# Unit 0's last fills shortened, one k load put off, unit 1's normalizations all on VectorE, weight loads held while unit 5's rows are transposed

## The chip, the cores and the metric

The kernel runs on one core of one Trainium2 chip. The metric is the device time of one execution in microseconds (us); the figure to compare is the median of several executions.

## The reference

Two layers, each a gated convolution followed by a gated feed-forward block, over 2048 tokens of width 576 in bfloat16:

```
x = x + A(layernorm(x));  x = x + B(layernorm(x))      # twice, the same weights
A(q) = q * (causal_conv(kv, ssm_k) + kv * ssm_D)       # by FFT over the 2048 tokens
       kv = (4-tap shift of A_k) * A_v
B(x) = (gelu(x @ w_gate) * (x @ w_up)) @ w_down        # 576 -> 4608 -> 576
```

kv does not depend on x, so the convolution's result y is computed once and used by both layers.

## The kernel before

**Tiles.** The tokens are cut into four blocks c of 512 (four rows-of-128, j = 0 to 3). A unit is one layer of one block: units 0 and 1 are layer 0 of blocks 0 and 1, units 2 and 3 layer 1 of the same blocks; units 4 and 5 are layer 0 of blocks 2 and 3, units 6 and 7 their layer 1. The passes over the weights are `[[0], [1, 2], [3, 4], [5, 6], [7]]`. Each pass has three phases (a third of the 4608 hidden columns each); a visit is one unit in one phase.

**A visit** is 12 gate/up groups (L1635: 18 products each of 64x512, gate and up into one PSUM pair), whose Gelu runs on ScalarE and whose product hT = gelu(gate) * up runs on VectorE (L1645), and then four row blocks of down products (L1669: 24 products each), each added to x_c by VectorE. In unit 0 VectorE is short of time, so while convolution work of block 1 is left, the groups go in twos: ScalarE takes both halves out of PSUM (L1542, L1543) and VectorE makes one 128x1024 product for two groups (L1546, in `hidden`). That product waits in the list `made` until `run_made` issues it. Unit 0's first phase takes its rows in two halves (`half_gu`).

**The convolution** of block m runs beside all this: transforms of k*v and of the filter on TensorE (the four steps of `quarter`, L292, for each half h of the columns; a step is two products), their evictions on ScalarE, complex products and sums on VectorE (the queue V), inverse transforms on TensorE (L416), and a spill of the spectra through HBM. `filt(m)` transforms block m of the filter, `step(m)` does the rest. Their TensorE work is the queue `Pq`, in order; it is offered within the down products, and within gate/up groups only where `now()` says so (for `quarter`, only the last two steps of the second half). y of block 1 is wanted by unit 1, y of block 2 by unit 4, y of block 3 by unit 5.

**A unit's rows** are made by `gate2_steps` (two VectorE operations a row, L1236 and L1243: x + (x - mean) * y * rstd), then a mean on GpSimd (L1193), a square on ScalarE (L1201), two small GpSimd operations for rstd (L1208, L1209), the normalization xn (on ScalarE, L1265, in `norm`; or on VectorE, L1273 and L1275, in `norm_v`), and two transposing DMAs on SyncE's queue (SP) into xnT (L1298, in `spread`). The unit's first gate/up product needs all four rows of xnT.

**The order** on every engine is written out by a planner: `Pace` keeps a time for TensorE, VectorE and ScalarE, moved on by constants (`C_GU` = 1.944 for a gate/up group, `C_DN` = 0.245 for two down products, and so on). After each group or pair of down products, `fill(limit, ...)` issues what is ready: weight loads (`weights`), loads of the convolution (`run_loads`), transposes (`spreads`), products in `made` that are ready, VectorE work as long as the planned VectorE time stays below `limit`, ScalarE work, and convolution steps on TensorE. `limit` is the planned TensorE time plus C_GU plus LEAD (1.8), or HURRY (2.6) while y of block 1 is unfinished. The engines then run their own lists in order, each at its own speed; a DMA that must wait holds up what is behind it on its queue.

**Weight loads** are entered with a due time (`when_due`) once the group that frees their buffer is planned: three DMAs (L1155 to L1157) on SP, the same queue as the transposes. `weights()` issues them all at once, except that while unit 1's rows are being made and turned, those due more than HOLD = 14 us ahead are kept back.

**k and v** of block 2 are loaded on GpSimd's queue (`lk` in `step`, L174). `conv.clear` lets `lk` and the steps of `filt` go as soon as all four of unit 1's rows have their transposes issued.

Of the kernel before, what the change touches and what calls it, by code (L numbers as in the profile page):

```python
# [26 lines left out]
RT = BS // P  # L27
# [4 lines left out]
NEVER = 1e9  # L32

C_GU, C_DN = 1.944, 0.245
# [7 lines left out]
AHEAD, CHAINED = 2.0, 2.5  # L42
LATE = (1, 2)
HOLD, LEAD, HURRY, SPARE = 14.0, 1.8, 2.6, 4.0


def twiddles():
# [1050 lines left out]
def ssm_geglu_kernel(ctx, tc, A_q, A_k, A_v, A_shift_k, A_ssm_k, A_ssm_D, B_x, B_w_gate, B_w_up,  # L1098
# [9 lines left out]
    FP = FT // NP  # L1108
# [13 lines left out]
    t = Pace()  # L1122
# [54 lines left out]
    aq, nq = deque(), deque()  # L1177
# [80 lines left out]
    def prep(ui, j):  # L1258
        layer, c = units[ui]
        v = nvars.setdefault(ui, [{"pfx": "l_"} for _ in range(RT)])[j]  # L1260

        def norm(ready):
            xn = xnp.tile([P, XW], BF16, tag="xn", name="xn")
            for lo, hi in ((0, D), (D, XW)):
                nc.scalar.activation(out=xn[:, lo:hi], in_=x_c[c][:, j, 0:hi - lo], func=ACT.Identity,  # L1265
                                     scale=v["rstd"][:, 0:1], bias=v["nb"][:, 0:1])
            xn_made.append((ui, j, xn, t.on_act(C_NA, max(ready, t.pe - 1.0)) + 0.3 - 2.0 * (ui == 1)))

        def norm_v(j):
            def run():  # L1270
                v = nvars[ui][j]
                xn = xnp.tile([P, XW], BF16, tag="xn", name="xn")
                nc.vector.tensor_scalar(out=xn[:, 0:D], in0=x_c[c][:, j, :], scalar1=v["nm"][:, 0:1],  # L1273
                                        scalar2=v["rstd"][:, 0:1], op0=ALU.add, op1=ALU.mult)
                nc.vector.tensor_copy(out=xn[:, D:XW], in_=xn[:, 0:HK])  # L1275
                xn_made.append((ui, j, xn, t.dve + C_NV - 1.7))
            return ("v", nvars[ui][j], "rstd_at"), C_NV, run
        tasks = gate2_steps(c, j, (hvars if layer else gvars)[c][j], v, layer == 1)
        if ui > 1 or j == 1:
            v["norm"] = norm  # L1280
        if ui == 1:
            tasks += [norm_v(i) for i in {1: (0,), 3: (2, 3)}.get(j, ())]
        return tasks

    hvars = {}
# [7 lines left out]
    xn_made = deque()  # L1293
# [11 lines left out]
        blk_of[2 * b + 1] = 5 + b  # L1305

    vq = deque()
    xnT_of, xn_done = {}, {}

    def run_vq(limit, till=0.0):  # L1310
        if not vq:
# [19 lines left out]
    def spreads():  # L1331
        while xn_made and xn_made[0][3] <= t.pe:
            ui, j, xn, _ = xn_made.popleft()
            if ui not in xnT_of:
                xnT_of[ui] = xtp.tile([P, NKC, CH], BF16, tag="xnT", name="xnT")
            spread(xnT_of[ui], j, xn)
            xn_done[ui] = xn_done.get(ui, 0) + 1

    due = []

# [3 lines left out]

    def turns_near():

        return bool(xn_made or nq) or 1 in xnT_of and xn_done.get(1, 0) < RT

    def weights():

        while due:
            near = turns_near() and xn_done.get(1, 0) < RT
            if near and due[0][0] > t.pe + HOLD:
                break
            _, _, load, n = due.pop(0)
            load(n)
# [19 lines left out]
    def fill(limit, tensor, conv_first):  # L1376
        weights()
        conv.run_loads()
        spreads()
        while made and made[0][0] <= max(t.pe + 0.2, t.dve):  # L1380
            run_made()
        while True:
            if conv_first:
                if not (conv.run_v(limit) or run_vq(limit)):
                    break
            else:
                done = run_vq(limit)
                if done is None or not (done or conv.run_v(limit)):
                    break
        while run_aq(min(limit, t.pe + 2.3)):  # L1390
            pass
        conv.flush(t.pe)
        if tensor and (hurry() or t.pe > conv.last + (CHAINED if chained() else 0.0)):
            for _ in range(3):
                if not conv.run_p():
                    break
        if unit0 and conv.borrowed:
            while run_vq(limit, t.pe + C_GU):
                pass

    with tc.manual_schedule():
# [133 lines left out]
        def hidden(dst, pair, e, count):  # L1535
# [11 lines left out]
                    out=dst, in0=ga[:].rearrange("p e (f q) -> p (e f) q", f=count), in1=dst, op=ALU.mult)))  # L1547
            return when + 0.1

        def half_gu(hT, n, half, old):  # L1550
            pair = psp.tile([P, 2, 512], F32, tag="pr", name="gu")
            xnT, tok = xnT_of[0], slice(half * 2 * P, (half + 1) * 2 * P)
            for e in range(2):
                w, gi = wgu[(2 * n + e) // FG], (2 * n + e) % FG
                for k in range(NKC):
                    for s, r0 in ((0, 0), (1, HK)):
                        nc.tensor.matmul(pair[:, s, e * 256:(e + 1) * 256], lhsT=w[r0:r0 + HK, k, gi * P:(gi + 1) * P],  # L1557
                                         rhs=xnT[r0:r0 + HK, blk_of[k], tok], start=(k == 0), stop=(k == NKC - 1))
            if not old:
                return lambda: hidden(hT[:, 4 * (n // 2):4 * (n // 2) + 4, tok], pair, n % 2, 2)  # L1560
            ga = work.tile([P, CH], F32, tag="ga", name="ga")
            nc.scalar.activation(out=ga[:], in_=pair[:, 0, :], func=ACT.Gelu_apprx_tanh)
            nc.vector.tensor_tensor(out=hT[:, 2 * n:2 * n + 2, tok], in0=ga[:].rearrange("p (e q) -> p e q", e=2),
                                    in1=pair[:, 1, :].rearrange("p (e q) -> p e q", e=2), op=ALU.mult)
# [20 lines left out]
            return kind is not None and need[0] == "y2" and need[1:3] not in conv.y_at  # L1585
        now = lambda: wanted() or hurry() and (t.pe > 60.0 or conv.fresh > 0)
        conv.tight, conv.turning = chained, turns_near
        conv.clear = lambda: 0.0 if xn_done.get(1, 0) >= RT else NEVER
        visits = []
        for pi, us in enumerate(passes):  # L1590
            visits += [(pi * NP + ph, ph, ui, k == 0, k == len(us) - 1)
# [1 line left out]
        for wb, ph, ui, first, final in visits:  # L1593
            layer, c = units[ui]
            while xn_done.get(ui, 0) < RT:
                if not run_vq(t.pe + 3.0):
                    conv.run_loads()
                    run_aq(t.pe + 3.0)
                    conv.run_v(t.pe + 1.5)
                    conv.run_p()  # L1600
                    t.pe += 0.2
                spreads()
            for kind, n in at_start.get((ui, ph), []):
                if kind == "es":
                    act_early(n)
                elif kind == "x":
                    load_x(n)
                else:
                    for j in range(RT):
                        vq.extend(prep(n, j))  # L1610
# [8 lines left out]
            if wb == 0:  # L1619
                first_half(hT)  # L1620
                for n in range(FP // 2):
                    tail = half_gu(hT, n, 1, False)
                    t.pe = max(t.pe, free.popleft()) + C_GU
                    free.append(tail())
                    if n % 2:
                        when_due(t.pe, load_wgu, n // 2 + 3)
                    fill(t.pe + C_GU + (HURRY if hurry() else LEAD), now(), conv.left > 0)
            for fi in range(FP if wb else 0):
                n, gi = divmod(wb * FP + fi, FG)
                w = wgu[n]  # L1630
                pair = psp.tile([P, 2, 512], F32, tag="pr", name="gu")
                for k in range(NKC):
                    b = blk_of[k]
                    for s, r0 in ((0, 0), (1, HK)):
                        nc.tensor.matmul(pair[:, s, :], lhsT=w[r0:r0 + HK, k, gi * P:(gi + 1) * P],  # L1635
                                         rhs=xnT[r0:r0 + HK, b, :], start=(k == 0), stop=(k == NKC - 1))
                t.pe = max(t.pe, free.popleft()) + C_GU
                if ui == 0 and (fi % 2 and rounded or fi % 2 == 0 and conv.left > 0):
                    rounded = True
                    free.append(hidden(hT[:, fi - fi % 2:fi - fi % 2 + 2, :], pair, fi % 2, 1))  # L1640
                else:
                    rounded = False
                    ga = work.tile([P, CH], F32, tag="ga", name="ga")
                    nc.scalar.activation(out=ga[:], in_=pair[:, 0, :], func=ACT.Gelu_apprx_tanh)  # L1644
                    nc.vector.tensor_tensor(out=hT[:, fi, :], in0=ga[:], in1=pair[:, 1, :], op=ALU.mult)  # L1645
                    free.append(t.on_dve(C_HT, t.on_act(C_GELU, t.pe + 0.15) + 0.15) + 0.1)
                if conv.borrowed:
                    free.popleft()
                    free.append(conv.borrowed)
                    conv.borrowed = None  # L1650
                if gi == FG - 1 and final:
                    when_due(t.pe + (FP - FG) * C_GU + 12.0, load_wgu, n + 3)
                fill(t.pe + C_GU + (HURRY if hurry() else LEAD), now(), conv.left > 0)
            conv.borrowed = None
            while made:
                run_made()
# [103 lines left out]
```

## Time and profile before

| | us |
|---|---|
| median of 3 runs (920.41 to 921.9) | 921.73 |
| the profiled execution, its own time | 919.29 |
| its span, first to last instruction | 917.5 |
| TensorE busy (98% of the span) | 902.6 |
| VectorE busy (63%) | 577.1 |
| ScalarE busy (36%) | 334.3 |
| GpSimd busy (17%) | 160.1 |
| granted TensorE clock | 1.0 throughout |

By the chain that ended last, an undisturbed gate/up of 12 groups takes 23.42 us and an undisturbed set of down products 11.87 us, with 0.49 us more for every four products of the convolution between them. The landmarks of that chain used below: unit 0's second phase begins at 80.42, its third at 117.25, that phase's down products at 144.94; unit 1's gate/up begins at 161.04, its down products at 184.69; unit 4's last phase begins at 560.38, its down products at 583.8; unit 5's gate/up begins at 595.59. All times in the texts are from the span's start.

### The profile page before, as it was taken

How to read it: one execution, taken by the hardware profiler on the slowest of the kernel's cores; microseconds unless marked ns; L12 is line 12 of the kernel's file. 1: busy time of each engine (PE TensorE's matmuls, PEld its weight loads, DVE VectorE, ACT ScalarE, POOL GpSimd, SP SyncE). 2: the span in 40 equal slices, each digit the busy share in tenths (PEclk: the TensorE clock that was granted, in tenths of full speed). 3: DMA queues.
4: the chain of work that ended last, by engine and by line, in shares of the span. 5: the costliest groups of instructions: out<-in, count | busy, mean ns of one | idle time of the engine just before them, and what ended most of it. 6: DMA issues, size and time to landing. Idle time of an engine off the chain costs nothing.

```text
span 917.5 us, 19235 instructions
## 1 busy us (share of the span) xinstructions
PE 902.6 (98%) x8166; PEld 526.5 (57%) x8166; DVE 577.1 (63%) x983; ACT 334.3 (36%) x628; POOL 160.1 (17%) x334
## 2 busy tenths in 40 slices
PE   8899998999999999999999999999999999999998
PEld 6786555465565564654655655656546556556555
DVE  7989877768889884697898865442332335332332
ACT  6865546523224145353124133551121224421211
POOL 3503405220114022340113002220000003100000
PEclk9999999999999999999999999999999999999999
DMA  9979997948518609893925802940720821977620
GB/s 253 332 198 281 246 251 122 207 155 168 181 53 202 167 1 151 239 155 83 277 68 118 192 16 59 179 126 5 151 78 2 155 79 27 164 174 174 138 63 27
DMA packets 128955, 131.15 MB, mean 143 GB/s; under 512 B 43618, under 2 KB 120675, under 8 KB 128868
## 3 DMA queue, kind: packets, MB, share of 16 engines
q1 hardware_dynamic: 119232, 93.47, 49.1%
q0 software_dynamic: 9632, 36.43, 12.3%
q8 instruction: 64, 1.05, 0.5%
q14 instruction: 23, 0.19, 0.1%
q10 hardware_dynamic: 4, 0.01, 0.0%
HBM read 108.35 MB, written 11.80 MB: 131 GB/s over the span
## 4 chain that ended last, share of the span: by engine, by line
PE 92%; DVE 3%; DMA 2%; ACT 1%; SPq 1%; POOL 1%; issue 0%; DVEq 0%; POOLq 0%; ACTq 0%
PE gu L1635 58%; PE dn L1669 28%; PE gu L1557 2%; DMA xnT<-xn 2%; PE ps L217 1%; PE cps L292 1%; PE ps L416 1%; PE cps L416 1%; SPq L1298 0%; PE ps L292 0%; DVE wx L948 0%; DVE x_c L1460 0%; DVE x_c L1457 0%; POOL rstd L1209 0%; PE cps L885 0%
## 5 line engine op out<-in xcount | busy, mean ns | idle before, releaser
L1635 PE MATMUL gu<-xnT,wgu 64*128 64x512 bf16 x4968 | 541.0, 376 | 4.1 <-DMA xnT<-xn 4.1
L1635 PEld LDWEIGHTS <-wgu 64*128 64x128 bf16 x4968 | 241.5, 94 | 297.0 <-issue 10.5
L1644 ACT ACTIVATE ga<-gu 128x512 f32<-128x512 f32 x258 | 154.0, 597 | 467.8 <-PE gu L1635 460.8
L1645 DVE TENSOR_TENSOR hT<-ga,gu 128x512 bf16<-128x512 f32 x258 | 177.0, 686 | 205.0 <-ACT ga L1644 203.5
L1669 PE MATMUL dn<-wd,hT 128*128 128x288 bf16 x2304 | 292.2, 286 | 1.4 <-DVE hT L1546 1.4
L1669 PEld LDWEIGHTS <-hT 128*128 128x128 bf16 x2304 | 223.4, 98 | 67.2 <-issue 9.5
L1705 DVE TENSOR_TENSOR x_c<-x_c,dn 128x576 f32<-128x576 f32 x64 | 48.1, 752 | 61.4 <-PE dn L1669 61.2
L1193 POOL TENSOR_SCALAR nm<-s 128x1 f32<-128x1 f32 x60 | 20.4, 340 | 273.4 <-DVE x_c L1700 210.9
L1201 ACT ACTIVATE junk<-x_c,nm 128x576 bf16<-128x576 f32 x48 | 36.9, 768 | 22.4 <-POOL nm L1193 21.0
L1209 POOL TENSOR_TENSOR rstd<-ve,neghalf_t 128x1 f32<-128x1 f32 x62 | 41.9, 676 | 5.2
L556 POOL DMA_DIRECT2D hr<-Hd x32 | 17.4, 545 | 123.5 <-DVE prod L375 122.3
L1208 POOL TENSOR_SCALAR ve<-ss 128x1 f32<-128x1 f32 x62 | 25.3, 408 | 57.5 <-ACT junk L1201 57.3
L1265 ACT ACTIVATE xn<-x_c,nb,rstd 128x576 bf16<-128x576 f32 (+1 forms) x50 | 29.7, 644 | 4.8 <-POOL nb L1213 4.8
L1691 DVE TENSOR_TENSOR ob<-x_c,dn 128x576 bf16<-128x576 f32 x15 | 11.3, 754 | 30.2 <-PE dn L1669 27.2
L1542 ACT ACTIVATE ga<-gu 128x512 bf16<-128x512 f32 x26 | 15.5, 597 | 33.4 <-PE gu L1635 26.4
L295 ACT COPY eo<-cps 128x576 f32<-128x576 f32 x29 | 18.6, 640 | 20.4 <-PE cps L292 16.8
L1557 PE MATMUL gu<-xnT,wgu 64*128 64x256 bf16 x432 | 24.6, 269 | 0.1
L431 POOL DMA_DIRECT2D out_dram<-ob x12 | 6.8, 565 | 94.4 <-DVE ob L1691 74.2
L376 DVE TENSOR_TENSOR prod<-prod 128x576 bf16<-128x576 bf16 x48 | 22.0, 458 | 1.7
L1557 PEld LDWEIGHTS <-wgu 64*128 64x128 bf16 x432 | 20.8, 94 | 3.5 <-issue 0.7
L255 DVE SCALAR_TENSOR_TENSOR eo<-eo 128x576 f32<-128x576 f32 x22 | 16.4, 752 | 4.7 <-ACT eo L295 4.7
L616 DVE TENSOR_TENSOR zs<-sum,prod 128x576 f32<-128x576 bf16 x24 | 18.1, 754 | 0.4
(164 smaller groups left out, 581.1 us busy)
## 6 DMA issues: line engine op xcount, KB each, us to landing
wgu<-in_B_w_gate_dram SPq DMA_DIRECT2D x45, 576.0 KB, 6.0
wd<-in_B_w_down_dram SPq DMA_DIRECT2D x30, 864.0 KB, 6.9
wgu<-in_B_w_up_dram SPq DMA_DIRECT2D x45, 512.0 KB, 7.9
hr<-Hd POOLq DMA_DIRECT2D x32, 288.0 KB, 5.0
kr<-Kd POOLq DMA_DIRECT2D x24, 288.0 KB, 5.4
Kd<-kc POOLq DMA_DIRECT2D x12, 288.0 KB, 7.3
k<-in_A_k_dram POOLq DMA_DIRECT2D x3, 1008.0 KB, 13.2
wgu<-in_B_w_up_dram SPq DMA_DIRECT2D x45, 64.0 KB, 7.4
```

The source lines that it names most:

```text
L376: nc.vector.tensor_tensor(out=dst, in0=pr[:, 0, :], in1=pr[:, 1, :], op=ALU.subtract if part == 0 else ALU.add)
L1193: nc.gpsimd.tensor_scalar(out=v["nm"][:], in0=v["s"][:], scalar1=-1.0 / D, scalar2=None, op0=ALU.mult)
L1201: nc.scalar.activation(out=junk[:], in_=get_x(), func=ACT.Square, bias=v["nm"][:, 0:1], accum_out=v["ss"][:])
L1208: nc.gpsimd.tensor_scalar(out=ve[:], in0=v["ss"][:], scalar1=1.0 / D, scalar2=EPS, op0=ALU.mult, op1=ALU.add)
L1209: nc.gpsimd.tensor_tensor(out=v["rstd"][:], in0=ve[:], in1=neghalf_t[:, 0:1], op=ALU.pow)
L1265: nc.scalar.activation(out=xn[:, lo:hi], in_=x_c[c][:, j, 0:hi - lo], func=ACT.Identity, scale=v["rstd"][:, 0:1], bias=v["nb"][:, 0:1])
L1557: nc.tensor.matmul(pair[:, s, e * 256:(e + 1) * 256], lhsT=w[r0:r0 + HK, k, gi * P:(gi + 1) * P], rhs=xnT[r0:r0 + HK, blk_of[k], tok], sta ...
L1635: nc.tensor.matmul(pair[:, s, :], lhsT=w[r0:r0 + HK, k, gi * P:(gi + 1) * P], rhs=xnT[r0:r0 + HK, b, :], start=(k == 0), stop=(k == NKC - 1))
L1644: nc.scalar.activation(out=ga[:], in_=pair[:, 0, :], func=ACT.Gelu_apprx_tanh)
L1645: nc.vector.tensor_tensor(out=hT[:, fi, :], in0=ga[:], in1=pair[:, 1, :], op=ALU.mult)
L1669: nc.tensor.matmul(part[h][:, h, 0:HW], lhsT=hT[:, fi, at * P:(at + 1) * P], rhs=wd[2 * wb + fi // WT][:, fi % WT, h * HW:(h + 1) * HW], s ...
L1705: nc.vector.tensor_tensor(out=xh, in0=xh, in1=acc[:, :, 0:HW], op=ALU.add)
```

## The change

Four parts, all in the planner's rules; no operation changes its shape.

1. **Ends of unit 0's gate/up.** `lead(left)` sets the limit of the fill: with a product in `made` and fewer than two groups left, VectorE may be filled only to 1.5 us (ENDING) past the planned TensorE time after the last group, where it was C_GU + 2.6 or 1.8. And the loop that issues unit 1's gating right after two inverse transforms (`conv.borrowed`) gets a limit of its own, C_GU + 1.6 (VISIT) counted from after those transforms, where it had the fill's limit, counted from before them.
2. **k of block 2** and the steps of `filt` wait until 9 us (LANDED) after unit 1's last row was issued for transposing (`xn_at`), in planned time.
3. **Row 1 of unit 1** is normalized by `norm_v` on VectorE, as rows 0, 2 and 3 are; it stands behind row 3's gating, ahead of rows 2 and 3.
4. **Weights held back also for unit 5**: from unit 4's last phase on, `turning` holds unit 5 too, and `weights()` and `turns_near()` go by the units in it whose rows are not all turned.

```diff
+LANDED, ENDING, VISIT = 9.0, 1.5, 1.6
...
-        if ui > 1 or j == 1:
+        if ui > 1:
             v["norm"] = norm
         if ui == 1:
-            tasks += [norm_v(i) for i in {1: (0,), 3: (2, 3)}.get(j, ())]
+            tasks += [norm_v(i) for i in {1: (0,), 3: (1, 2, 3)}.get(j, ())]
...
             xn_done[ui] = xn_done.get(ui, 0) + 1
+            xn_at[ui] = t.pe
...
-        return bool(xn_made or nq) or 1 in xnT_of and xn_done.get(1, 0) < RT
+        return bool(xn_made or nq) or any(u in xnT_of for u in left_to_turn())
+
+    turning = [1]
+
+    def left_to_turn():
+        return [u for u in turning if xn_done.get(u, 0) < RT]
...
         while due:
-            near = turns_near() and xn_done.get(1, 0) < RT
+            near = turns_near() and left_to_turn()
             if near and due[0][0] > t.pe + HOLD:
                 break
...
         if unit0 and conv.borrowed:
-            while run_vq(limit, t.pe + C_GU):
+            while run_vq(t.pe + C_GU + VISIT, t.pe + C_GU):
                 pass
...
+        def lead(left):
+
+            if made and left < 2:
+                return ENDING + left * C_GU
+            return C_GU + (HURRY if hurry() else LEAD)
...
-        conv.clear = lambda: 0.0 if xn_done.get(1, 0) >= RT else NEVER
+        conv.clear = lambda: xn_at[1] + LANDED if xn_done.get(1, 0) >= RT else NEVER
...
+            if (ui, ph) == (4, 2):
+                turning.append(5)
...
-                    fill(t.pe + C_GU + (HURRY if hurry() else LEAD), now(), conv.left > 0)
+                    fill(t.pe + lead(FP // 2 - 1 - n), now(), conv.left > 0)
...
-                fill(t.pe + C_GU + (HURRY if hurry() else LEAD), now(), conv.left > 0)
+                fill(t.pe + lead(FP - 1 - fi if ui == 0 else FP), now(), conv.left > 0)
```

More of the change, by code (lines that the diff above doesn't have):

```diff
@@ L1307, in ssm_geglu_kernel @@
     vq = deque()
-    xnT_of, xn_done = {}, {}
+    xnT_of, xn_done, xn_at = {}, {}, {}
     def run_vq(limit, till=0.0):
```

## The prediction

> **What bounds the kernel now.** I read the page first: TensorE is busy for 902.6 of 917.5 us at a granted clock of 1.0, so time comes only from its idle stretches or from the work in its list, and the change takes no product away. So I asked next for what TensorE waits for. Two rows after the opening 45 us matter:
>
> ```profile
> PE gu L1635 <- DMA xnT<-xn: 4.1, 2, 3.2
> PE dn L1669 <- DVE hT L1546: 1.4, 1, 1.4
> ```
>
> Three waits in all: two on transposed rows, one on VectorE. The chain of waits in order of time places them, and busy time over windows cut at its landmarks prices them (columns: window, length, busy PE, PEld, DVE, ACT, POOL, then clock, DMA share, GB/s):
>
> ```profile
> 80.42:117.25 36.83, 35.46 (x315) 19.66 (x316) 32.37 (x56) 18.63 (x40) 14.35 (x25) 1.00 1.11 291
> 144.94:157.86 12.92, 12.92 (x106) 10.09 (x104) 9.45 (x22) 9.35 (x20) 7.18 (x19) 1.00 0.86 134
> 157.86:161.04 3.18, 0.00 (x0) 0.03 (x1) 1.41 (x4) 0.55 (x2) 1.59 (x4) 1.00 0.52 114
> 161.04:184.69 23.65, 23.64 (x217) 10.51 (x218) 17.76 (x30) 12.83 (x25) 6.31 (x13) 1.00 0.96 195
> 560.38:583.80 23.42, 23.42 (x217) 10.44 (x218) 14.09 (x24) 13.92 (x27) 6.59 (x17) 1.00 0.68 131
> 595.59:620.12 24.53, 23.66 (x218) 12.26 (x218) 11.51 (x21) 13.62 (x27) 6.19 (x17) 1.00 0.48 122
> 620.12:631.99 11.87, 11.87 (x99) 9.32 (x100) 2.95 (x4) 0.60 (x1) 0.00 (x0) 1.00 0.00 0
> ```
>
> An undisturbed gate/up is 23.42, undisturbed down products 11.87. So unit 0's second phase loses 36.83 - 35.29 = **1.54**; from 144.94 to 184.69 are 39.75 against 23.42 + 11.87 + 0.98 (eight convolution products in between), **3.48** lost; unit 5 loses 24.53 - 23.42 = **1.11**. The sum, 6.13 us, is the most that this change can bring.
>
> **Part 1, the ends of gate/up.** The timeline at the end of unit 0's second phase:
>
> ```profile
> 104.37 0.58 ACT L1543 CAST hT<-gu 128x512 bf16<-128x512 f32 x1
> 104.52 1.43 DVE L390 TENSOR_TENSOR yb<-zs 128x576 bf16<-128x576 f32 x2
> 105.86 0.75 DVE L373 TENSOR_TENSOR prod<-kr,H 128x1152 bf16<-128x1152 bf16 x1
> 107.03 0.68 DVE L1546 TENSOR_TENSOR hT<-ga,hT 128x1024 bf16<-128x1024 bf16 x1
> 107.76 9.48 PE L1669 MATMUL dn<-wd,hT 128*128 128x288 bf16 x76 [1.37 <-DVE hT L1546]
> ```
>
> ScalarE is done with the last pair at 104.95, but VectorE first does 2.5 us of convolution (L390, L373, L376). With 1.5 us of fill the product goes at 104.95 and ends at 105.65; TensorE needs it after 20 down products, at 106.39. The wait goes whole: **-1.54**. The 2.5 us move behind the product; no VectorE work is added, and VectorE stood idle in those down products for 0.76 and 0.98 us waiting for TensorE (L1705) and 0.89 at 121.5 (for ScalarE), which takes up the 1.5 us that TensorE gains on it. If that cover is short, the chain to the inverse transforms (L397 ends at 129.83, the transforms start at 132.83: 3.0 us to spare, 1.6 after the gain) would miss its place by one group, 1.95 us. In the first phase's end the same rule only reorders; no wait stands there.
>
> The second half of this part: after the first pair of inverse transforms VectorE does row 0's gating, then waits 1.16 us (to 137.68) for Gelu, though y of row 1 is out at 135.65; after the second it waits 1.11 (to 141.86). Counted from after the transforms (1.96 us by the planner's constant) with 1.6 instead of 2.6, the limit is 0.96 later, room for one more 0.82 operation each time. Rows 1 to 3 come up to 1 us sooner. The hT product behind them slips by some 0.4 us; it frees a PSUM pair wanted two groups later.
>
> **Part 3, row 1's norm.** ScalarE loses two L1265 (1.19 us together), GpSimd one L1213 (0.19); VectorE gains L1273 and L1275, 0.57 + 0.18. Behind row 3's gating it would run at 146.9 to 147.7 (VectorE is idle there, 1.17 us to 148.09), 1 us after ScalarE's. Queued behind it: rows 2 and 3's norms, which start no later than now (148.78 and 149.48, behind L1705's sister L1700 at 148.09), and sooner if anything, since their squares no longer wait behind L1265. Eight transposing DMAs remain, 1.27 us each on SP: row 1 147.7 to 150.2, row 2 to 152.7, row 3 to 155.3.
>
> **Part 2, k of block 2.** SP's and GpSimd's rows, and DMA around them:
>
> ```profile
> 140.77 15.96 SPq L1298 DMA_TRANSPOSE xnT<-xn  x8
> 151.66 0.64 POOL L174 DMA_DIRECT2D k<-in_A_k_dram  x1
> 152.00:154.00 2.00, 2.00 (x18) 1.60 (x17) 1.67 (x5) 1.09 (x3) 0.87 (x4) 1.00 1.10 93
> 154.00:156.00 2.00, 2.00 (x19) 1.58 (x17) 1.14 (x3) 1.15 (x3) 1.75 (x5) 1.00 0.94 339
> ```
>
> Rows 0 and 1 land 2.5 to 2.6 us after issue. The second DMA of row 2 (issued 150.84) took 6.9 and the last (154.30) 7.1, its issue 2.43 instead of 1.27, while k's 1008 KB moved at 339 GB/s. With k away, the last DMA, issued near 154.0, lands by 156.5. The down products then end at 144.94 + 11.87 = 156.81, for the filter's steps leave too: the 3.48 go whole, margin 0.3, or about 1.3 with the sooner rows. Bounds: 3.48 down to 1.5, if the last rows land as slowly as 5 us.
>
> [...] In the two windows above the rate says that k had nearly all; the trace speaks against an even split here.
>
> What is moved: eight filter products (0.98 us) from 150 to 155 into unit 1's down products from 184.69, which then hold sixteen. Unit 2's, from 220.95 to 234.78, hold sixteen now and take 13.83 = 11.87 + 1.96, no wait. Zero. k was landed at 160.15 and first used at 174.49; issued from 158.8 with a landing of 8.5 to 13.4 (its three issues), it is there by 172.2: 2.3 to spare (on GpSimd's queue it only goes behind the x_b load of 159.29); gone, VectorE waits with hT products behind it. The v load (GpSimd, 188.03) waits for the filter's second half, some 6.5 us later now (two halves take 9.4 from 221.14 to 230.5, one 2.5), and v is used at 200.86: the convolution of block 2 slips by 4 to 8 us. Its last shift (L397) ends at 325.03; the filter's next half begins at 328.95 in down products that last to 342.59. It still gets in.
>
> **Part 4, unit 5.**
>
> ```profile
> 576.06 0.61 SPq L1155 DMA_DIRECT2D wgu<-in_B_w_gate_dram  x1
> 578.75 6.68 SPq L1298 DMA_TRANSPOSE xnT<-xn  x4
> 585.53 0.60 SPq L1155 DMA_DIRECT2D wgu<-in_B_w_gate_dram  x1
> 587.59 9.79 SPq L1298 DMA_TRANSPOSE xnT<-xn  x4
> ```
>
> Row 1's xn is ready at 573.93, but SP stands waiting for the weights' buffer till 576.06 and turns the row at 578.75; row 3's, ready at 581.69, goes at 587.59 behind another load and lands 8 us later. Held back, rows 2 and 3 go at 579.7 to 584.9 and land by 593 even with that 8: **-1.11**. The weights: due 27.55 us after the freeing group, kept until 14 before; the first is then issued about 13.5 us late in the planner, 10 or more before its use, landings being 6.0 to 7.9.
>
> **Sum**: -1.54 - 3.48 - 1.11 = -6.13, so the profiled 919.29 becomes 913.2. The median shown stands 2.44 above that execution; I carry the difference over: 921.73 - 6.13 = 915.6, and with some 0.3 for small new waits, **915.9**.
>
> **Rivals.**
> (a) *The last rows still land late.* For it: three causes must all go (k, SP's 1.27 each, the order in VectorE), the margin is 0.3 to 1.3, and z could miss its place by one group. [...]
> (b) *Nothing gained*: the planner's new order shifts the waits elsewhere, 920.5 to 922.5. Against it: each wait has one named releaser that the change touches.
> (c) *Slower, by the convolution.* If block 2's chain slips by more than 17 us (325.03 to 342.59), the filter's half falls to the next down products, 365.94, 37 us on. Then block 3's last shift comes at 576 instead of 538.93 and misses the down products of 546.55; its inverse transforms run in unit 4's last gate/up, unit 5's gating begins at 577 instead of 563.70, 13.3 later. The rows' last landing, 587 to 593 by part 4, becomes 601 to 606, 5 to 11 after the 595.59 at which TensorE wants them, while 5.0 of the gain stay: 921.8 to 927.4, say 925. For it: the sixteen products and v's wait. Against it: I get 4 to 8 of the 17.
> (d) *The hold does nothing* for unit 5: 1.11 stay, within the forecast's range.
>
> **Numbers.** Forecast (and d), 914.3 to 917.2: 0.58. (a) to 919.5: 0.20. (b): 0.08. (c): 0.14. The lower end is the full sum (915.6) less 1.3, what the lowest run shown lies below the median: 914.3. The range reaches through (a) to the faster edge of (b), 920.8. About 0.2%, 1.84 us, is what a measurement can tell from no change: faster 0.78, same 0.08, slower 0.14.
>
> **What would show it.** The row of waits for L1546 is gone and hT is made right after the last L1543; unit 1's gate/up begins right at the end of the down products, k's issue behind the last transpose; four L1273 where three stood and 48 L1265 where 50; unit 1's down products take 13.8; SP's transposes of unit 5 lie together, weights behind. I am wrong if a new wait of over 1 us stands in TensorE's rows, above all one on xnT near 590 or on y's chain.

## The result and the profile after

| | median us | lowest to highest | executions |
|---|---|---|---|
| before | 921.82 | 920.41 to 921.93 | 4 |
| after | 913.81 | 913.24 to 914.72 | 4 |

The ratio is 0.9918, with a 95% interval of 0.99 to 0.9935: 8.0 us, or 0.8%, less. The median lies 2.1 below the 915.9 of the forecast and 0.5 below the lower end of its range. The changed kernel's profiled execution took 914.25, its span 912.5, at a mean granted clock of 0.998.

All that TensorE waits for in the changed kernel, over the whole span (line that waits, line it waits for, us in total, times, longest):

```profile
PE xps L1436 <- DVE xn L1420: 2.7, 1, 2.7
PE cps L241 <- DVE v L943: 1.3, 1, 1.3
PE cps L886 <- DVE wx L864: 1.2, 1, 1.2
PE ps L899 <- ACT sx L901: 0.7, 1, 0.7
```

These four lie in the first 36 us and were there before. The rows on xnT and on hT are gone: behind the opening, TensorE waits for nothing any more. The windows that answer to those of before (unit 0's second phase; its last down products; unit 1's gate/up; its down products; unit 5's gate/up; line numbers have moved by 15, so L1650 is the gate/up and L1684 the down products):

```profile
81.21:116.49 35.28, 35.28 (x314) 19.68 (x316) 32.19 (x55) 18.61 (x40) 15.32 (x25) 1.00 1.08 292
...
144.25:156.12 11.87, 11.87 (x100) 9.29 (x100) 8.15 (x20) 6.10 (x14) 6.29 (x16) 1.00 0.57 78
156.12:179.54 23.42, 23.42 (x218) 10.46 (x218) 15.73 (x28) 13.17 (x27) 7.25 (x19) 1.00 1.01 245
179.54:193.36 13.82, 13.82 (x114) 10.86 (x116) 10.13 (x19) 5.31 (x9) 0.78 (x2) 1.00 0.15 44
...
591.49:614.91 23.42, 23.42 (x217) 10.46 (x218) 11.43 (x21) 13.62 (x27) 6.17 (x17) 1.00 0.89 170
```

Every stretch now has the undisturbed length: 36.83 became 35.28, unit 5's 24.53 became 23.42, and unit 1's gate/up starts where the down products end. From the start of those down products to the end of unit 1's gate/up it is 179.54 - 144.25 = 35.29 instead of 39.75; 0.98 of the difference came back as the filter's eight products in unit 1's down products, 13.82 instead of 12.84. So 1.55 + 3.48 + 1.11 = 6.14 were taken out of TensorE's time, to within 0.01 of the forecast's sum.

VectorE at the end of unit 0's second phase (start, duration, line):

```profile
104.65 0.76 DVE L617 TENSOR_TENSOR zs<-sum,prod 128x576 f32<-128x576 bf16 x1
105.77 0.69 DVE L1553 TENSOR_TENSOR hT<-ga,hT 128x1024 bf16<-128x1024 bf16 x1 [0.37 <-ACT hT L1550]
106.38 1.42 DVE L391 TENSOR_TENSOR yb<-zs 128x576 bf16<-128x576 f32 x2
107.72 0.75 DVE L374 TENSOR_TENSOR prod<-kr,H 128x1152 bf16<-128x1152 bf16 x1
```

The last hT no longer stands behind L391, L374 and the product that follows: it waits 0.37 for ScalarE, and they come after it. SyncE's queue ahead of unit 5:

```profile
567.77 6.17 SPq L1299 DMA_TRANSPOSE xnT<-xn  x4
574.04 0.64 SPq L1156 DMA_DIRECT2D wgu<-in_B_w_gate_dram  x1
574.73 0.62 SPq L1157 DMA_DIRECT2D wgu<-in_B_w_up_dram  x1
575.40 0.63 SPq L1158 DMA_DIRECT2D wgu<-in_B_w_up_dram  x1
576.13 7.01 SPq L1299 DMA_TRANSPOSE xnT<-xn  x4
583.24 0.60 SPq L1156 DMA_DIRECT2D wgu<-in_B_w_gate_dram  x1
```

Two groups of four transposes with one set of weights between them, where two sets stood (the forecast had none); the last is issued by 583.2, 8.3 before unit 5 begins. One thing does not fit, though: the two profiled executions differ by only 919.29 - 914.25 = 5.0, less than the 6.14 taken out (0.79 of it is lost ahead of unit 0's second phase, which begins at 81.21 and not at 80.42), while the medians differ by 8.0. That gap is what the experiments had to explain.

### The profile page after: what moved, and what is told of

It is laid out like the page before. It is cut to its first block, busy times and chain, and to the rows that moved or that the text cites. A ratio compares the mean times of both kernels' runs of the same rounds, so it can differ in the third digit from the quotient of the medians.

```text
span 912.5 us, 19232 instructions
## 1 busy us (share of the span) xinstructions
PE 903.1 (99%) x8166; PEld 525.6 (58%) x8166; DVE 577.4 (63%) x985; ACT 333.0 (36%) x626; POOL 160.0 (18%) x333
## 3 DMA queue, kind: packets, MB, share of 16 engines
q8 instruction: 64, 1.05, 0.5%
## 4 chain that ended last, share of the span: by engine, by line
PE 98%; DVE 1%; ACT 0%; issue 0%; DVEq 0%
PE gu L1650 59%; PE dn L1684 31%; PE gu L1570 3%; PE cps L293 1%; PE ps L417 1%; PE ps L218 1%; PE cps L417 1%; PE ps L293 0%; DVE wx L949 0%; PE xps L1436 0%; PE cps L886 0%; DVE wx L952 0%; PE cps L218 0%; DVE x_c L1467 0%; DVE x_c L1464 0%; PE ps L963 0%
## 5 line engine op out<-in xcount | busy, mean ns | idle before, releaser
L1650 PE MATMUL gu<-xnT,wgu 64*128 64x512 bf16 x4968 | 540.7, 377 | 0.0
L1650 PEld LDWEIGHTS <-wgu 64*128 64x128 bf16 x4968 | 240.3, 94 | 293.7 <-issue 5.9
L1684 PE MATMUL dn<-wd,hT 128*128 128x288 bf16 x2304 | 292.3, 287 | 0.0
L1684 PEld LDWEIGHTS <-hT 128*128 128x128 bf16 x2304 | 223.1, 98 | 65.9 <-issue 9.5
```

What stands on the lines that cost most here:

```text
L1684: nc.tensor.matmul(part[h][:, h, 0:HW], lhsT=hT[:, fi, at * P:(at + 1) * P], rhs=wd[2 * wb + fi // WT][:, fi % WT, h * HW:(h + 1) * HW], s ...
```

## The experiments

Every kernel here was timed beside the kernel before on the same chip, and the ratios are against that. Four chips were used in all; on them the kernel before's executions with a mean granted clock of 0.996 have medians from 921.16 to 922.12, so a difference of less than 1 us between two kernels timed on different chips is not sure. Line numbers differ a little from kernel to kernel.

**The kernel before, again.** Twice, unaltered: 12 executions (b1) and a single one (b2). Two theories of the 2.44 between the profiled execution and the median were put to it.

> The kernel before once more, unchanged, for a second profile of it and for what its executions differ by. The profiled execution of before took 919.29, the median 921.8. Theory V (the waits vary): a second profiled execution shows the same three waits, of another length, above all the one on xnT at unit 1 (3.2 in the first) or unit 5 (0.9), and an execution near 922 has 2 to 2.5 more there. Theory S (the start): the three waits are the same within 0.3 and the 2 us lie in the first 66 us, by a granted clock under 1 there, as the changed kernel's profile has at 36 to 39 us. Ratio to before 0.998 to 1.002 by both.

> The kernel before a third time, one look. V: the wait on xnT at unit 1 is again another, between 3 and 6. S: all three waits as in the first profile within 0.3, the first 66 us differ.

Measured: b1 921.51 median (917.25 to 923.53, 12 executions), ratio 0.9993 (0.9979 to 1.0008), profiled 922.14 at a clock of 0.996; b2 922.06, profiled, clock 0.996. TensorE's waits are nearly those of the first profile: 3.7 and 3.5 at unit 1 where it had 3.2, 0.5 and 0.8 at unit 5 where it had 0.9, 1.4 for hT in both. That is at most 0.5 more at unit 1 where theory V asked for 2 to 2.5 more in all, so V falls. The clock is what differs. Windows of b1 behind the wait at unit 1 (the column behind POOL's count is the granted clock):

```profile
157.00:160.40 3.40, 0.80 (x7) 0.39 (x5) 2.16 (x4) 1.35 (x4) 1.79 (x5) 1.00 1.31 50
160.40:163.80 3.40, 2.32 (x12) 1.03 (x14) 0.00 (x0) 0.00 (x0) 0.00 (x0) 0.50 1.17 217
163.80:167.20 3.40, 3.40 (x19) 1.41 (x16) 0.96 (x2) 1.35 (x3) 0.16 (x1) 0.50 1.10 226
```

The same window in the kernel before's first profile:

```profile
163.80:167.20 3.40, 3.40 (x34) 1.56 (x32) 3.03 (x6) 2.32 (x6) 2.01 (x6) 1.00 1.10 224
```

TensorE is "busy" for 3.40 us in both, but it gets through 19 products in the one and 34 in the other. The trace's clock record has b1 at half clock from 160.42 for 6.83 us, b2 from 162.21 for 3.41 and, at the start, from 35.92 for 3.41; the first profile has no such stretch ahead of the last products. b1's unit 1 gate/up took 26.31, b2's 25.17, against 23.64 in the first profile and 23.42 undisturbed. Theory S, which put the loss into the first 66 us, holds for one of b2's two stretches and for none of b1's. So the profile that the forecast was worked out from was the uncommon case.

**k held back alone, and everything but k.** `only_k` is the kernel before with part 2 alone, `no_k` the changed kernel without it:

```diff
# only_k, on the kernel before
+LANDED = 9.0
...
+            xn_at[ui] = t.pe
...
-        conv.clear = lambda: 0.0 if xn_done.get(1, 0) >= RT else NEVER
+        conv.clear = lambda: xn_at[1] + LANDED if xn_done.get(1, 0) >= RT else NEVER
# no_k, on the changed kernel: the last line back
```

> Before with part 2 alone (k of block 2 and the filter's steps 9 us after unit 1's last row). If k's transfer is what holds the last rows: unit 1's wait of 3.2 (5 or more in a typical execution) falls below 0.7, the last row's transposes land 2.5 to 3 after issue; time 3 to 5 below before. If the rows come late by themselves (the rival): 1.5 or more of the wait stays and the time is within 2 of before. The waits of 1.37 on hT and 0.87 at unit 5 stay in both.

> After without part 2: k and the filter's steps go as soon as unit 1's rows are issued. If k is the cause: the wait on xnT at unit 1 comes back, 2 to 4 us, and the time is 916 to 918. If the sooner rows (parts 1 and 3) are enough: no wait over 0.5, time 913 to 914.5, and in that case part 2 buys nothing.

Measured: only_k 917.18 (915.75 to 917.62, 5 executions), ratio 0.9955 (0.9939 to 0.9971); no_k 918.51 (915.93 to 919.89, 10), ratio 0.9966 (0.9954 to 0.9979). no_k's median lies 0.5 above the range expected of it; it has a half-clock stretch at the start and one at unit 1. only_k has no wait at unit 1 left; no_k has one of 3.5, and the stretch from 161.44 for 3.41 behind it. What the transposes issued from 148.0 on (146.8 in only_k, 147.1 in no_k) took to land (min, median, max), for the kernel before, then only_k, then no_k:

```profile
L1298 SPq DMA_TRANSPOSE xnT<-xn x5: 1199/1265/2433, 148.0 to 154.3; - x5
...
DMA to landing us min/median/max: 2.5/6.9/7.1
```

```profile
L1299 SPq DMA_TRANSPOSE xnT<-xn x6: 1199/1261/2148, 146.8 to 154.4; - x6
...
DMA to landing us min/median/max: 2.5/2.5/4.1
```

```profile
L1299 SPq DMA_TRANSPOSE xnT<-xn x5: 1201/1264/2735, 147.1 to 154.0; - x5
...
DMA to landing us min/median/max: 2.5/7.5/7.6
```

The issue times hardly differ, the landings do: with k's 1008 KB in flight on GpSimd's queue the last transpose lands 7.1 (before) and 7.5 (no_k) after its issue at 154.3 and 154.0, without it (only_k, issued at 154.4) 2.5, and the slowest 4.1. That is why rival (a) did not come: k was the cause of nearly all of the wait, as the forecast had it, and not of a part of it. The rate that the prediction read this from does not show it by itself, since the transposes have few bytes to move. The trace also has the packets: between 150 and 156.8 in the kernel before, k's queue moved 0.98 MB in 135 of them and SyncE's 0.33 MB in 1353, so one packet of k holds as much as 30 of a transpose (7.3 KB against 0.24). No run tests whether the slow landings have to do with that. Part 2 is the larger half of the change.

**The other parts, each left out of the changed kernel.** `no_hold` without part 4, `no_lead` without the smaller fill, `no_rows` without the limit VISIT and without row 1's norm on VectorE:

```diff
# no_hold
-            if (ui, ph) == (4, 2):
-                turning.append(5)
# no_lead
-            if made and left < 2:
-                return ENDING + left * C_GU
# no_rows
-        if ui > 1:
+        if ui > 1 or j == 1:
-            tasks += [norm_v(i) for i in {1: (0,), 3: (1, 2, 3)}.get(j, ())]
+            tasks += [norm_v(i) for i in {1: (0,), 3: (2, 3)}.get(j, ())]
-            while run_vq(t.pe + C_GU + VISIT, t.pe + C_GU):
+            while run_vq(limit, t.pe + C_GU):
```

> The changed kernel without its fourth part: unit 5's weights are not held back. Theory C (the prediction's three waits, and a half-clock stretch of 3.41 us only behind a TensorE idle of some 3 us): unit 5's wait of 1.1 us comes back and nothing else, since 1.1 us of idle is too short to bring a slow stretch: 914.8 to 915.0 median. Rival 1: any wait brings a slow stretch, then 1.1 + 1.7 = 2.8 more, 916.6. Rival 2: the rows of unit 5 come early enough without the hold, then 913.8 and no wait.

> The changed kernel without the smaller fill at the ends of unit 0's gate/up. Theory C: the wait of the down products for the last hT of unit 0's second phase is back, 1.4 us, with no slow stretch behind it: 915.2 to 915.4 median. Rival 1 (any wait brings a slow stretch): 1.4 + 1.7, 916.9. Rival 2: the new order of VectorE's work (the visits) already takes the convolution's operations out of that place, then no wait and 913.8.

> The changed kernel with unit 1's rows made as in the kernel before (row 1's norm on ScalarE, no longer limit after the inverse transforms), k still held back. Theory C: the kernel before with k alone held back waited 0.6 us here, so 0.3 to 0.7 come back and no slow stretch follows: 914.1 to 914.5 median. Rival: the sooner rows carry the gain of unit 1's start, then 1.5 to 3 us of wait and, often, a slow stretch: 915.5 to 918.5.

| | median us | ratio (95%) | at clock 1.0 | at 0.998 |
|---|---|---|---|---|
| no_hold | 913.79 | 0.9927 (0.991 to 0.9944) | 913.70, 913.77, 913.81 | 915.28 |
| no_lead | 916.01 | 0.9945 (0.9928 to 0.9963) | 914.56 | 915.89, 916.14, 916.63 |
| no_rows | 914.17 | 0.9927 (0.9909 to 0.9946) | | 914.12, 914.12, 914.21, 914.86 |

These medians of four can't be set side by side, for the clock varies among them; read down the columns, against the changed kernel's 913.24 to 913.37 and 914.10 to 914.79 (below). The changed kernel's figures come from other chips. no_lead loses 1.2 at 1.0 and 1.7 at 0.998, and this row is back in its profile:

```profile
PE dn L1682 <- DVE hT L1553: 1.4, 1, 1.4
```

No half-clock stretch stands behind that wait, only the one at the start (from 34.73), as theory C has it; its median was off, for theory C left out that the stretch at the start comes in some executions and not in others.

no_hold has the old order on SyncE's queue again, weights between the transposes:

```profile
580.39 0.60 SPq L1156 DMA_DIRECT2D wgu<-in_B_w_gate_dram  x1
...
582.46 9.66 SPq L1299 DMA_TRANSPOSE xnT<-xn  x4
```

Yet TensorE waits only 0.2 there, and 0.3 to 0.6 are lost at clock 1.0 (913.70 to 913.81 against 913.24 to 913.37, on different chips). In seven profiled executions with the old order this wait was 0.9, 0.5, 0.8, 0.6 (only_k), 0.2 here, and 0 and 0.7 in the two runs that follow; the 1.11 that the forecast took belongs to the longest of them. Theory C's 1.1 did not come back, and the median is rival 2's; that a small wait stays is all that speaks against rival 2. The hold is worth something between that 0.2 and about half of what was forecast. no_rows loses nothing that can be told: no wait at unit 1 and 914.12 to 914.86 at 0.998, the changed kernel's own spread. Its median is in theory C's range, but not for theory C's reason, since the 0.3 to 0.7 of wait did not come back. With k out of the way the sooner rows were not needed.

**The wait filled, not removed.** If the half-clock stretch is brought by TensorE's idling, giving it something to do while it waits must take the stretch away and leave the wait. `warm28` and `warm12` put 28 and 12 spare products at the head of unit 1's gate/up in the kernel before; the first real group overwrites what they made (the diff is warm28's):

```diff
+                if (ui, ph, fi) == (1, 0, 0):
+                    for i in range(28):
+                        nc.tensor.matmul(pair[:, i % 2, :], lhsT=w[i % 2 * HK:i % 2 * HK + HK, 0, 0:P],
+                                         rhs=xnT_of[0][i % 2 * HK:i % 2 * HK + HK, 0, :], start=True, stop=True)
                 for k in range(NKC):
```

> The kernel before with 28 spare products (64 rows by 512 columns, 0.108 us each, 3.0 us in all) at the head of unit 1's gate/up, on rows that are there already; the group that follows overwrites them. The wait for unit 1's rows stays as long as it is. Theory C (slow stretches come from TensorE's idling): the half-clock stretch near 160 to 167 us is gone and the mean clock rises from 0.996 to 0.998 or 1.0; median 919.3 to 920.3 (1.5 to 2.5 below the kernel before), though no wait is removed. Rival V (the stretches are not brought by the idle, or cost nothing): 921.8, clock 0.996. Third way: the spare products end later than the rows land, up to 0.3 us slower than theory C.

> As the run with 28 spare products at the head of unit 1's gate/up, with 12 of them: 1.3 us of the wait is filled and some 1.9 us of TensorE idle stays. Theory C1 (the slow stretch follows an idle of about 3 us or more): it is gone here too, median 918.0 to 919.0 (start's stretch aside). Theory C2 (any idle of over 1 to 2 us can bring it, by chance): some executions keep it, clocks of 0.996 and 0.998 among them, median 919.0 to 920.5. Rival V: 920.7 to 921.8, as the kernel before.

Measured: warm28 918.23 (917.89 to 919.92, 10 executions), ratio 0.9978 (0.9967 to 0.9989), where the kernel before beside it had 920.68. Its seven executions at clock 1.0 took 917.89 to 918.32, the three others (0.997 and 0.998) up to 919.92; none is at 0.996. Windows of its profile, the wait and then unit 1's gate/up:

```profile
157.60:160.80 3.20, 3.18 (x29) 1.26 (x28) 1.46 (x4) 0.60 (x2) 1.59 (x4) 1.00 0.42 97
160.80:184.72 23.92, 23.66 (x217) 10.50 (x218) 17.76 (x30) 12.83 (x25) 6.30 (x13) 1.00 1.01 195
```

The gate/up ends at 184.72, where it ended in the first profile (184.69): the rows came no sooner, and still 2.45 us are gone from the median. That is theory C, and rival V falls. (The 918.23 itself lies below theory C's 919.3 to 920.3, which was reckoned from a kernel before of 921.8.) Not all of the 2.45 is the clock. At clock 1.0 warm28 has a median of 918.03, and the kernel before beside it 918.64 in three executions; in warm28's profile the wait at unit 5 is missing as well. So some 1.8 are the clock's, as an estimate from these two medians.

With 12 spare products, 919.2 (917.28 to 921.19, 10 executions), ratio 0.9986 (0.9973 to 0.9999): six at clock 1.0, four at 0.998. In its profile TensorE idled 2.1 at unit 1 and kept its clock there (1.00 in unit 1's gate/up); its one half-clock stretch lies at the start, from 34.88. The three others at 0.998 have no trace that would say where theirs was. The median lies 0.2 above C1's range and in C2's; that none is at 0.996, and that six are at 1.0, favours C1, and C2 is not excluded.

**The start filled.** The changed kernel has one wait of that size left, 2.69 ahead of the first turning of rows, and its profile shows what follows it:

```profile
36.00:39.40 3.40, 3.40 (x22) 2.37 (x19) 1.74 (x5) 1.99 (x4) 0.00 (x0) 0.51 0.99 367
```

`start_m` fills it with spare products, `start_t` with more transposes of the identity:

```diff
# start_m
+            spare = small()
+            for _ in range(22):
+                nc.tensor.matmul(spare[:, 0, 0:256], lhsT=self.W[:, 0, :], rhs=self.W[:, 0:2, :], start=True, stop=True)
             head.turn(0, 8)
# start_t
-            head.turn(0, 8)
+            head.turn(0, 40)
```

> The changed kernel with 22 spare products (128 rows by 256 columns, some 0.11 us each, 2.4 us in all) ahead of the first turning of rows near 31.6 us, where TensorE idles for 2.7 us and then often runs at half clock for 3.41 us. Theory C: the stretch at 35 to 39 us is gone in all executions, clock 1.0; median 913.0 to 913.4, the changed kernel's best execution. Rival: 2.7 us of idle is too short and the stretch comes from something else; then 913.8 with clocks of 0.998 as often as now.

> The same place filled with 32 more transposes of the identity (0.077 us each, 2.5 us) in place of products. Theory C with transposes counting as work: as with products, clock 1.0, 913.0 to 913.4. Theory that transposes do not hold the clock: 913.8 to 914.5, a stretch at half clock near 35 to 39 us in half of the executions or more.

Measured: start_m 913.29 (913.2 to 913.64), ratio 0.9922 (0.9899 to 0.9945); start_t 913.27 (913.05 to 913.36), ratio 0.9921 (0.9893 to 0.9948). All eight executions have a clock of 0.999 or 1.0. The same window in start_m, then in start_t:

```profile
36.00:39.40 3.40, 3.40 (x41) 2.52 (x41) 2.35 (x7) 2.64 (x5) 0.00 (x0) 1.00 1.04 388
```

```profile
36.00:39.40 3.40, 3.40 (x44) 2.55 (x43) 2.35 (x6) 2.63 (x5) 0.00 (x0) 1.00 1.05 385
```

Twice the products in the same 3.40 us; transposes keep the clock here as products do, in four executions of each. About 1 us of the changed kernel's median goes with it (913.27 over the eight executions, against 914.26 of its ten), and its spread, 1.5 us, shrinks to 0.6. Both are faster than the kernel before; whether they are faster than the changed one by that 0.1% is open, since they were not timed side by side.

**The changed kernel, again**, for its executions' clocks.

> The changed kernel again, unaltered, timed in five rounds, for its executions' times and mean clocks. Theory C: it has no clock below 0.998 (only the stretch behind the start's 2.7 us of idle is left); its executions at 1.0 take 913.2 to 913.4, some 6.1 below the kernel before at 1.0 (919.3), as the three waits summed to, and those at 0.998 take 914.2 to 914.8; the kernel before beside it has a median of 920.7 to 921.8 at 0.996. Rival: the further gain over the three waits is in work, not in the clock; then executions at 1.0 lie 7 to 8 below the kernel before at 1.0.

Measured: 914.33 (913.35 to 914.79, 6 executions), ratio 0.9927 (0.991 to 0.9943), the kernel before beside it at 920.68. The execution times by mean granted clock, over all comparisons that list it, all chips together:

| clock | before: executions, us (median) | after: executions, us (median) |
|---|---|---|
| 0.999 or 1.0 | 9, 917.25 to 919.75 (919.15) | 3, 913.24 to 913.37 (913.35) |
| 0.998 | 24, 918.36 to 921.48 (920.44) | 7, 914.10 to 914.79 (914.40) |
| 0.996 | 37, 920.82 to 922.90 (921.85) | none |
| 0.994 | 4, 922.87 to 923.85 (923.41) | none |

One stretch of 3.41 us at half clock takes 0.5 x 3.41 / 915 = 0.002 off the mean clock, so the column counts them: the kernel before most often has two, the changed one none or one. At equal clock the change brings 5.8 (at 1.0) and 6.0 (at 0.998), and not the 7 to 8 of the rival; on a2's chip alone it is 6.2 at 0.998, by six executions against five. The rest is the stretches that are gone, 1.3 to 1.6 from row to row in the kernel before. In the changed kernel, where only the one at the start is left, the step is 1.05.

## Why the prediction was right and wrong

**The step that failed** is "The median shown stands 2.44 above that execution; I carry the difference over". The 2.44 was not a constant of the measurement. The profiled execution had the clock at 1.0 throughout, as 9 of 74 later executions of that kernel had. The median, 921.73, has the time of an execution with two half-clock stretches (the row of 0.996 above; its own clock is not on record), and in b1 both of them, in b2 one, stand behind the very wait that the change removes. The sum against the execution's own time was 913.2, and the changed kernel's three executions without a stretch took 913.24 to 913.37. That it fits to 0.2 is in part luck, since the kernel before's nine executions at clock 1.0 span 2.5 us. With the one stretch that stays at the start the changed kernel takes 914.1 to 914.8. So of the 2.44 that were carried over, 0.6 was there in the median (913.81 less 913.2): a stretch at unit 1, worth 1.3 to 1.75 (the table's rows; b2's 25.17 against 23.42), goes with the wait, and the one at the start was missing in two of the four executions. The 0.3 for new waits did not come either. The range's lower end had the same fault: it took 1.3 from three executions' spread, and 74 span 6.6 us. How far below it the result fell was chance: all ten executions of the changed kernel have a median of 914.26, right at that end and still 1.6 under the forecast.

**The three terms.** -1.54 measured 1.55 in the profile, and 1.2 to 1.7 by no_lead. -3.48 measured 3.48 in the profile, and only_k's one execution at clock 1.0 lies 3.4 below the 919.15. -1.11 measured 1.11 in the profile pair, but it was one execution's wait; no_hold gives 0.3 to 0.6 between chips, and 0.2 in its profile. That the parts taken singly at clock 1.0 make some 5 of 5.8 is within the 2.5 us by which the kernel before's own executions at 1.0 differ; what moves those was not settled.

**Rows.** They came sooner by 1.2 (the last transpose issued at 153.1, not 154.3). The last landed 2.5 after issue, at 155.6, the slowest took 4.0, and the down products ended at 156.12: a margin of 0.5, not 1.3. But only_k and no_rows have no wait at unit 1 either, so holding k back was enough by itself, if barely (only_k: landed at 156.9, wanted at 156.93). Row 1's norm and the visits cost and bring nothing that can be told.

**What was moved** did fit in at zero. k landed at 160.92 + 11.2 = 172.1 and was first used at 173.0: 0.9 to spare, not 2.3. The slip of block 2 was put at 4 to 8 and measured 1.7 (v's load at 189.7 for 188.03, its use at 202.5 for 200.86), since all sixteen filter products found a place in unit 1's down products, up to 189.4, and those began 5 us sooner. Rival (c) needed 17 and was far off: the filter's next half went at 327.88 within the same down products.

**The other rivals.** (b) fell with the first profile; (d) is half true, as no_hold shows.

## What to carry to other kernels

A wait of some 3 us on TensorE (2.69 to 3.68) costs more than its length here: a stretch at half clock often follows, worth another 1.05 to 1.75 each in these kernels. So when a profiled execution lies below the median, compare granted clocks before carrying the difference over: if the change removes such a wait, the difference goes too. Where a wait can't be removed, spare products in it can bring back the second part (some 1.8 of 920.68 here, by the estimate from warm28); and a large load that isn't urgent is better issued after small transfers that TensorE waits for (here the last transpose landed 2.5 us after its issue with k's 1008 KB put off, and 7.1 with it in flight).

## What was not expected of the hardware

By the length of a wait no sharp threshold of the clock shows here: 2.69 us of idle at the start was followed by half clock in the changed kernel's profiles and not in the first profile of the kernel before, which also kept full clock through 3.18 at unit 1, where 3.5 and 3.7 lost it for 3.41 and 6.83 us. With 2.1 (warm12) and 0.9 (start_t) of idle left, the profiles show no such stretch behind it.

The clock records show more. In the two kernels' first profiles the clock changes only at whole multiples of 3.413 us behind the record's first entry: after 8, 9 and 265 in the changed kernel's, after 266 in the other, which lies behind the last product; in b2 the two stretches begin 126.29 us apart, 37 times that length. So the windows below have that length, counted from the first entry or from the start of a half-clock stretch. TensorE's idle time within them, from the same traces:

| profile | wait | window, us | idle in it, us | clock in the next window |
|---|---|---|---|---|
| after | 2.69, start | 32.62 to 36.03 | 2.25 | 0.5 |
| before | 2.69, start | 33.08 to 36.49 | 1.99 | 1.0 |
| before | 3.18, unit 1 | 155.96 to 159.37 | 1.51 | 1.0 |
| | | 159.37 to 162.78 | 1.67 | 1.0 |
| b1 | 3.68, unit 1 | 157.01 to 160.42 | 2.62 | 0.5 |
| b2 | 3.49, unit 1 | 158.79 to 162.21 | 3.33 | 0.5 |
| warm12 | 2.08, unit 1 | 161.17 to 164.59 | 1.71 | 1.0 |

In this table half clock follows the three windows with 2.25 us of idle or more, and none of the four with 1.99 or less. (In b1 the window that follows, at half clock and with 1.07 of idle, is followed by half clock once more: hence 6.83, two windows.) Whether a limit lies between the two, and where, was not measured. By this table the same wait costs a stretch or not by how it falls across the windows: the first profile's 3.18 was cut nearly in half, 1.51 and 1.67, and no stretch shows behind it.

The same kernel thus runs in steps, with medians of 919.15, 920.44, 921.85 and 923.41 by the number of stretches, and a median of four can move by a step. Within a step its executions still differ by up to 3.1 us; the wait at unit 5 was between 0 and 1.1 in the profiles, and the rest of that is open.
